# Attention loads of a fused attention and expert kernel issued one or two slots later in program order

## Chip, core and metric

The kernel runs on one core of one Trainium2 chip. The metric is the device time of one execution in microseconds (us), given as the median of several runs. Matrix products run on TensorE (PE in the profile), elementwise work on VectorE (DVE), ScalarE (ACT) and GpSimd (POOL). SyncE (SP) computes nothing here: it issues almost all DMA transfers, one after the other in program order, and an issue that has to wait holds up every issue behind it.

## What is computed

The reference is a chunked attention followed by two products of gated linear layers without activation functions:

```python
for c in range(nc):                      # 24 chunks of 32 queries, per batch (4) and head (8)
    q_c = q[:, :, c_start:c_end]
    k_full = np.concatenate([mem_k, k_ctx], axis=2)   # 8 memory keys, then 16 left, 32 own, 8 right
    v_full = np.concatenate([mem_v, v_ctx], axis=2)
    scores = scale * np.matmul(q_c, k_full.transpose(0, 1, 3, 2))
    scores = scores - np.max(scores, axis=-1, keepdims=True)
    a = np.exp(scores)
    a = a / (np.sum(a, axis=-1, keepdims=True) + 1e-09)
    out[:, :, c_start:c_end] = np.matmul(a, v_full)
x = attention output as 3072 tokens x 512
y = (((x @ w1) * (x @ w2)) @ w3) @ w_out           # 512 -> 1024 -> 512
result = ((y @ w_a) * (y @ w_b)) @ moe2_w_out      # 512 -> 1536 -> 512
```

All of it is float32. The dense products use operands split into a high and a low part and three passes.

## The kernel before

**Stages.** The first stage (up to about 81 us) decodes w3 and w_out, which arrive as raw words, and multiplies them into one matrix (`wps`, two halves of 32 products each, lines 566 to 603). The second stage goes over six tiles of 512 tokens (`ti`, line 705): for each of eight blocks `m` the products psA and psB with w1 and w2 (`ab_step`), then psY with the folded matrix. Beside it, the weights w_a and w_b are decoded, combined and stored to DRAM (`c_weights`, tiles `co`, `wc`). The third stage, from about 535 us on, is the second expert layer, a product with seven multiplications (`seven`) and the output product.

**Attention** has 16 units `u` (line 284). A unit is cut into steps, and each has a slot number: `BASE[u]` plus an offset. Per unit: `a_k` (line 110) loads the keys to `kraw`, `a_q` (line 120) the queries to `q`, `a_v` (line 129) the values to `v` in four DMAs (eight in the first unit of a batch), all on SP. `a_keys` (line 146) copies `kraw` into overlapping windows `kw` on DVE. `a_scores` (line 160) is the product `sc` on PE, `a_max` the row maximum `mx` on DVE, `a_exp` (line 196) 16 exponentials on ACT, `a_norm` the division on DVE and POOL, `a_trans` and `a_pt` the transposition `pt` and its copy, `a_pv` (line 237) the product `xp` with `v`, and `a_x` (line 256) the split of its result into `xt` (lines 99 and 102). Every one of `kraw`, `kw`, `q` and `v` has a single buffer. So q(u+1) can be loaded only after the scores of u have been computed, k(u+1) only after the copy of the keys of u, and v(u+1) only after the product xp(u).

**Order.** The order is written out by hand. `at` (line 281) puts steps into the list `todo[slot]`, and `attn_slot` (line 312) emits the next slot's steps, in the order of that list. In the first stage a slot is emitted every second product from `g` 9 of half 0 on: slots 0 to 6 in half 0, slots 7 to 22 in half 1. After the slot, `w_tick` (line 432) may follow: it decodes a weight block and issues loads of raw weights for as long as a buffer is free (`w_load`, line 350; tiles `raw`, sources `in_w3a`, `in_w3b`, then `in_w`). In half 0 this happens at `g` 0, 2, 4, 6, 8 and 9. In the second stage `between` (line 640) emits the due slots and then one `w_tick`, or one step of `c_weights`, whose loads (line 464, `in_wab`) and stores (line 493) are on SP as well. Within a slot's list, entries stand in the order in which the loop over `u` made them.

The framework adds the waits. Beside those for data and buffers, there is one for the eight completion semaphores that the DMAs of SP and ACT take in turn: a DMA whose semaphore still belongs to an unfinished transfer, eight issues back, waits for that.

Of the kernel before, what the change touches and what calls it, by code (L numbers as in the profile page):

```python
# [45 lines left out]
def tile_attention_moe(  # L46
# [60 lines left out]
    def new_batch(u):  # L107
        return NE * u % NG == 0
# [11 lines left out]
    def a_q(u):  # L120
        if u >= NA:
            return
        q = qs[u] = att.tile([P, NE, 4 * GQ], F32, tag="q", bufs=1, name="q")
        src = qt[2 * NE * u : 2 * NE * u + 2 * NE]
        nc.sync.dma_start(
            out=q, in_=src.rearrange("(e r) d h q -> (r d) e (h q)", r=2)
        )

    def a_v(u):
        if u >= NA:  # L130
            return
        for r in range(2):
            for e in range(NE):
                src = vw[2 * NE * u + 2 * e + r]
                kd, x = src.ap
                if new_batch(u):
                    mem = bass.AP(src.tensor, src.offset, [[kd[0], NMEM], [0, NC], x])
                    nc.sync.dma_start(out=v[D * r : D * r + NMEM, e, :, :], in_=mem)
                win = bass.AP(
                    src.tensor,  # L140
                    src.offset + NMEM * kd[0],
                    [[kd[0], KEYS - NMEM], [CHUNK * kd[0], NC], x],
                )
                nc.sync.dma_start(out=v[D * r + NMEM : D * r + D, e, :, :], in_=win)
# [51 lines left out]
    def a_exp(i):  # L196
        def stage_of(u):
            sc, t, mx, sm = soft[u]
            for a in range(2 * i, 2 * i + 2):
                for r in range(2):  # L200
                    nc.scalar.activation(  # L201
                        t[:, a, r, :],
                        sc[:, r, a, :],
                        AF.Exp,
                        bias=mx[:, r, a : a + 1],
                        scale=SCALE,
                        accum_out=sm[:, a, r : r + 1],
                    )

        return stage_of  # L210

    def a_norm(e):
        def stage_of(u):
            t, mx, sm = soft[u][1:]
            t, sm = t[:, 4 * e : 4 * e + 4], sm[:, 4 * e : 4 * e + 4]
            nc.vector.tensor_scalar_add(sm, sm, 1e-9)
            nc.vector.reciprocal(sm, sm)  # L217
            nc.gpsimd.tensor_tensor(  # L218
                t, t, sm[:, :, :, None].to_broadcast([GQ, 4, 2, KEYS]), ALU.mult
            )  # L220

        return stage_of
# [52 lines left out]
    BASE = [0, 6, 13, 23, 29, 36]  # L275
# [5 lines left out]
    def at(s, *stages):  # L281
        todo.setdefault(s, []).extend(stages)

    for u in range(NA):
        t0, t1, t2, t3 = SLOTS.get(u, (6, 7, 8, 9) if u < NX else (5, 5, 6, 7))
        for s, stage_of in (
            (t0, a_trans),
            (t1, a_pt),
            (t3, a_x),
            (t2, a_pv),  # L290
            (t2, lambda u: a_v(u + 1)),
            (0, a_scores),
            (0, lambda u: a_q(u + 1)),
            (int(u > 0), a_max),
            (2, a_norm(0)),
            (2 + (u > 0), a_norm(1)),
            (int(u > 0), a_exp(0)),
            (int(u > 0), a_exp(1)),
            (2 * (u > 0), a_exp(2)),
            (2 * (u > 0), a_exp(3)),  # L300
        ):
            at(BASE[u] + s, (stage_of, u))
        if u > 0:
            at(BASE[u] - 3, (a_keys, u), (a_k, u + 1))
    at(0, (a_v, 0))
    NEED = []
    for i in range(NT1):
        u = -(-TT * (i + 1) // (NE * GQ)) - 1
# [721 lines left out]
```

## Time and profile before

| | us |
|---|---|
| median of 3 runs (1075.88 to 1077.11) | 1076.02 |
| the profiled execution's own time | 1074.61 |
| its span, first to last instruction | 1072.8 |
| PE busy | 1055.9 |
| DVE busy | 452.1 |
| ACT busy | 443.3 |
| POOL busy | 233.3 |

A busy PE is not PE at its peak, since ends of matmuls are modelled; stretches in which PE is not busy are real gaps. An entry such as `[1.30 <-DVE w_f L378]` says that the engine was idle for 1.30 us before this instruction, until DVE had written `w_f` in line 378. `SPq` is the queue of SP: its times are those of issuing, and a transfer lands later.

### The profile page before, as it was taken

The page shows a single profiled execution, that of the slowest core. Times are in us where ns is not written, and L with a number is a line of the kernel's source. Part 1 is how long each engine was busy: PE and PEld are TensorE (multiplying, and loading weights), DVE is VectorE, ACT ScalarE, POOL GpSimd, SP SyncE. Part 2 cuts the span into 40 slices and gives each one's busy share as a digit, 9 for nine tenths or more (in the row PEclk, how much of TensorE's full clock was granted, in tenths as well). Part 3 has the DMA queues.
Part 4 walks back from the last instruction along what each step waited for, and adds up shares of the span by engine and source line. Part 5 has one row for each costly group of instructions (what it writes and reads, how often), then busy time and mean ns, then how long its engine had stood idle before and what let it go on. Part 6 is the DMA issues. An engine that isn't in the chain of part 4 may idle for free.

```text
span 1072.8 us, 18442 instructions
## 1 busy us (share of the span) xinstructions
PE 1055.9 (98%) x7442; PEld 844.5 (79%) x7442; DVE 452.1 (42%) x751; ACT 443.3 (41%) x1153; POOL 233.3 (22%) x228
## 2 busy tenths in 40 slices
PE   9999899999999999999999999999999999999998
PEld 3447688888888888888888888888888888888886
DVE  4667644435435435346643434432322253223310
ACT  6777754426636543535433343332222232222210
POOL 0102312202303302212033222112233202222210
PEclk9999999999999999999999999999999999999999
DMA  9966464454454462263555554523344434433311
GB/s 366 315 174 185 132 186 142 130 164 149 150 187 116 141 188 91 104 235 138 196 200 210 202 182 158 186 97 148 137 151 178 158 111 141 172 139 138 137 40 39
DMA packets 62341, 172.02 MB, mean 160 GB/s; under 512 B 6320, under 2 KB 21552, under 8 KB 56368
## 3 DMA queue, kind: packets, MB, share of 16 engines
q1 hardware_dynamic: 51680, 104.75, 30.2%
q0 software_dynamic: 10368, 66.06, 17.0%
q8 instruction: 58, 0.95, 0.4%
q14 instruction: 27, 0.22, 0.1%
q10 hardware_dynamic: 208, 0.04, 0.0%
HBM read 137.27 MB, written 33.55 MB: 159 GB/s over the span
## 4 chain that ended last, share of the span: by engine, by line
PE 86%; DVE 1%; DMA 1%; ACT 0%; issue 0%; POOL 0%; SPq 0%; ACTq 0%; POOLq 0%
PE ps L816 31%; PE ops L90 18%; PE psY L90 12%; PE psB L90 11%; PE psA L90 10%; PE xp L90 2%; PE sc L90 1%; PE pt L229 1%; DMA raw<-in_wab 1%; DVE x L102 0%; DVE tmp L670 0%; POOL g L635 0%; ACT x L99 0%; POOL t L218 0%; DVE xt L102 0%
## 5 line engine op out<-in xcount | busy, mean ns | idle before, releaser
L816 PE MATMUL ps<-x,w 128*128 128x512 f32 x1512 | 348.7, 389 | 0.3 <-ACT tmp L828 0.3
L816 PEld LDWEIGHTS ps<-x,w 128*128 128x128 f32 x1512 | 283.6, 188 | 60.1 <-ACT tmp L828 1.4
L833 DVE TENSOR_TENSOR tmp<-ps,tmp 128x512 f32<-128x512 f32 x108 | 74.6, 691 | 260.7 <-PE ps L816 230.6
L90 PE MATMUL psA<-xt,w 128*128 128x512 f32 x576 | 140.9, 393 | 3.8 <-DVE w L408 3.0
L90 PE MATMUL psB<-xt,w 128*128 128x512 f32 x576 | 140.0, 392 | 0.0
L90 PE MATMUL psY<-g,wo 128*128 128x512 f32 x576 | 136.0, 392 | 0.3 <-POOL g L635 0.3
L635 POOL TENSOR_TENSOR g<-gv,g 128x512 fp32r<-128x512 f32 x48 | 65.0, 1354 | 301.5 <-ACT g L634 301.5
L828 ACT ACTIVATE tmp<-ps 128x512 f32<-128x512 f32 x108 | 64.5, 597 | 157.5 <-PE ps L816 157.5
L90 PEld LDWEIGHTS psA<-xt,w 128*128 128x128 f32 x576 | 107.0, 188 | 28.0 <-DVE w L408 3.8
L90 PEld LDWEIGHTS psY<-g,wo 128*128 128x128 f32 x576 | 107.0, 188 | 23.1 <-POOL g L635 0.8
L90 PEld LDWEIGHTS psB<-xt,w 128*128 128x128 f32 x576 | 107.2, 188 | 22.5
L700 POOL DMA_DIRECT2D w<-wc x72 | 39.6, 552 | 373.3 <-PE ps L816 373.2
L90 PE MATMUL ops<-wo,g 128*128 128x512 f32 x504 | 118.6, 389 | 0.0
L90 PEld LDWEIGHTS ops<-wo,g 128*128 128x128 f32 x504 | 94.6, 188 | 19.6
L839 ACT ACTIVATE g<-tmp 128x512 fp32r<-128x512 f32 x66 | 40.7, 633 | 140.2 <-DVE tmp L838 140.2
L840 POOL TENSOR_TENSOR g<-tmp,g 128x512 fp32r<-128x512 f32 x66 | 84.0, 1291 | 20.8 <-ACT g L839 19.7
L201 ACT ACTIVATE t<-sc,mx 96x64 f32<-96x64 f32 x256 | 75.3, 316 | 25.0 <-DVE mx L193 23.4
L90 PE MATMUL ops<-fo,g 128*128 128x512 f32 x288 | 68.2, 389 | 0.0
L90 PEld LDWEIGHTS ops<-fo,g 128*128 128x128 f32 x288 | 54.1, 188 | 11.2
L218 POOL TENSOR_TENSOR t<-t,sm 96x512 f32<-96x512 f32 x32 | 37.2, 1163 | 104.6 <-DVE sm L217 100.3
L90 PE MATMUL wps<-w_f 128*128 128x512 f32 x128 | 57.6, 600 | 1.9 <-DVE w_f L378 1.9
L201 ACT ACTIVATION_READ_ACCUMULATOR t<-sc,mx 96x1 f32 x256 | 53.9, 211 | 0.0
(65 smaller groups left out, 870.3 us busy)
## 6 DMA issues: line engine op xcount, KB each, us to landing
w<-wc POOLq DMA_DIRECT2D x36, 1024.0 KB, 7.0
w<-wc POOLq DMA_DIRECT2D x36, 768.0 KB, 5.1
wc<-co SPq DMA_DIRECT2D x84, 256.0 KB
raw<-in_wab SPq DMA_DIRECT2D x24, 512.0 KB
v<-in_vw SPq DMA_DIRECT2D x64, 168.0 KB
kraw<-in_kt SPq DMA_DIRECT2D x16, 512.0 KB
raw<-in_w SPq DMA_DIRECT2D x16, 512.0 KB
raw<-in_w3a SPq DMA_DIRECT2D x6, 1024.0 KB
```

Source lines behind the costliest of these rows:

```text
L90: nc.tensor.matmul(o, lhsT=l, rhs=r, start=first, stop=last)
L201: nc.scalar.activation(t[:, a, r, :], sc[:, r, a, :], AF.Exp, bias=mx[:, r, a : a + 1], scale=SCALE, accum_out=sm[:, a, r : r + 1],)
L218: nc.gpsimd.tensor_tensor(t, t, sm[:, :, :, None].to_broadcast([GQ, 4, 2, KEYS]), ALU.mult)
L229: nc.tensor.transpose(pt[:, a // 4, a % 4, :], t[:, a].rearrange("p r k -> p (r k)"), id_sb)
L635: nc.gpsimd.tensor_tensor(g2[:, 1, :], gv, g2[:, 0, :].bitcast(F32), ALU.subtract)
L700: nc.gpsimd.dma_start(out=t[:, c0:c1].bitcast(F32), in_=src[:, c0:c1])
L816: nc.tensor.matmul(ps, lhsT=w[:, i, a, k, :], rhs=xs[i][:, b, k, :], start=first and n == 0, stop=n == 5, skip_group_check=not first,)
L828: nc.scalar.activation(z, ps, AF.Copy)
L833: nc.vector.tensor_tensor(z, ps, y, ALU.add)
L839: nc.scalar.activation(g2[:, 0, :], z, AF.Copy)
L840: nc.gpsimd.tensor_tensor(g2[:, 1, :], z, g2[:, 0, :].bitcast(F32), ALU.subtract)
```

## The change

Three calls change their place in the list of slots, and nothing else changes. The query load of unit u+1 moves from slot `BASE[u]` to `BASE[u] + 1`, or `+ 2` for u > 0. The value load moves from slot `BASE[u] + t2` to `BASE[u] + t2 + 1`, or `+ 2` for u > 1. The key load moves from `BASE[u] - 3` to `BASE[u] - 2`.

```diff
@@ -288,9 +288,7 @@
             (t1, a_pt),
             (t3, a_x),
             (t2, a_pv),
-            (t2, lambda u: a_v(u + 1)),
             (0, a_scores),
-            (0, lambda u: a_q(u + 1)),
             (int(u > 0), a_max),
             (2, a_norm(0)),
             (2 + (u > 0), a_norm(1)),
@@ -301,7 +299,10 @@
         ):
             at(BASE[u] + s, (stage_of, u))
         if u > 0:
-            at(BASE[u] - 3, (a_keys, u), (a_k, u + 1))
+            at(BASE[u] - 3, (a_keys, u))
+            at(BASE[u] - 2, (a_k, u + 1))
+        at(BASE[u] + 1 + (u > 0), (a_q, u + 1))
+        at(BASE[u] + t2 + 1 + (u > 1), (a_v, u + 1))
     at(0, (a_v, 0))
```

## Rows read from the trace of the kernel before

**Rows 1.** Waits of PE, 0 to 200 us: us in total, times, longest.
```profile
PE psA L90 <- DVE w L408: 3.0, 2, 2.2
PE pt L229 <- DVE xt L102: 2.5, 1, 2.5
...
PE psY L90 <- POOL g L635: 0.3, 1, 0.3
```

**Rows 2.** Waits of SP's queue over the whole span, same columns.
```profile
SPq L144 <- PE xp L90: 54.1, 23, 13.5
```

**Rows 3.** Timeline of SP's queue, 30 to 41 us: start, us, line, transfer, count.
```profile
30.08 0.39 SPq L125 DMA_DIRECT2D q<-in_qt  x1
...
38.27 0.27 SPq L138 DMA_DIRECT2D v<-in_vw  x1
40.10 0.32 SPq L144 DMA_DIRECT2D v<-in_vw  x1
40.52 0.36 SPq L357 DMA_DIRECT2D raw<-in_w3b  x1
```

**Rows 4.** Waits of SP's queue, 28 to 50 us.
```profile
SPq L138 <- DMA raw<-in_w3b: 3.8, 2, 3.2
...
SPq L144 <- DMA q<-in_qt: 1.5, 1, 1.5
```

**Rows 5.** Windows, busy us by engine; the last three columns: PEclk, DMA share, GB/s.
```profile
41.00:43.00 2.00, 0.70 (x40) 0.54 (x27) 1.97 (x3) 0.01 (x1) 0.00 (x0) 1.00 0.96 250
43.00:46.00 3.00, 3.00 (x8) 1.33 (x8) 1.56 (x3) 1.31 (x9) 0.00 (x0) 1.00 0.97 392
```

**Rows 6.** Timeline of PE, 39 to 58 us.
```profile
39.27 0.83 PE L229 MATMUL pt<-id_sb,t 96*128 96x96 f32 x8
40.22 1.18 PE L90 MATMUL sc<-kw,q 64*32 64x64 f32 x96
42.71 5.42 PE L90 MATMUL wps<-w_f 128*128 128x512 f32 x12 [1.30 <-DVE w_f L378]
...
57.50 0.85 PE L229 MATMUL pt<-id_sb,t 96*128 96x96 f32 x8 [2.50 <-DVE xt L102]
```

**Rows 7.** Timeline of DVE, 43 to 57 us.
```profile
43.17 1.21 DVE L192 TENSOR_REDUCE mx<-sc 96x16 f32<-96x1024 f32 x1
...
56.40 0.96 DVE L102 TENSOR_TENSOR xt<-xp,xt 128x768 fp32r<-128x768 f32 x1 [1.32 <-ACT xt L99]
```

**Rows 8.** Windows: PE, PEld, DVE, ACT, POOL, PEclk, DMA share, GB/s.
```profile
44.70:58.60 13.90, 11.40 (x125) 5.79 (x125) 7.62 (x11) 13.90 (x43) 2.08 (x2) 1.00 0.74 233
```

**Rows 9.** Windows at the end, same columns.
```profile
1066.00:1068.00 2.00, 1.82 (x9) 1.16 (x7) 1.21 (x2) 0.68 (x2) 0.00 (x0) 1.00 0.32 119
...
1070.00:1071.00 1.00, 0.00 (x0) 0.00 (x0) 0.00 (x0) 0.00 (x0) 0.00 (x0) 0.63 0.21 78
```

**Rows 10.** Timeline of SP's queue, 67 to 77 us.
```profile
67.45 1.94 SPq L144 DMA_DIRECT2D v<-in_vw  x4
71.53 4.90 SPq L357 DMA_DIRECT2D raw<-in_w  x3
```

**Rows 11.** Timeline of PE, the third unit's xp.
```profile
77.50 1.60 PE L90 MATMUL xp<-p,v 64*64 64x32 f32 x96
```

**Rows 12.** The chain that ended last, in order of time, 131 to 138 us.
```profile
131.08 0.40 SPq L125
...
131.57 6.63 DMA raw<-in_wab
```

**Rows 13.** Timeline of SP's queue in the steady part.
```profile
258.35 1.94 SPq L144 DMA_DIRECT2D v<-in_vw  x4
...
263.60 7.99 SPq L493 DMA_DIRECT2D wc<-co  x4
```

**Rows 14.** Timeline of PE in the steady part, the next xp.
```profile
280.29 1.60 PE L90 MATMUL xp<-p,v 64*64 64x32 f32 x96
```

**Rows 15.** Windows: ACT is the fourth busy column.
```profile
110.00:120.00 10.00, 10.00 (x134) 8.36 (x133) 4.62 (x10) 10.00 (x43) 2.52 (x2) 1.00 0.59 160
```

## Prediction

> **What bounds the kernel now.** I read the page's busy times first: PE is busy for 1055.9 us of a span of 1072.8 (the table above), so nothing that leaves PE's gaps alone changes the time. Next, PE's waits. Everything that the attention loads could touch lies in the first 150 us, and it is little: 3.0 us for split weights (`w`, line 408), 2.5 us before the second transposition, 0.3 us before psY [rows 1], and 1.30 us before the second half of the fold [rows 6]. Third, SP's own waits: its issues of `v` stood for 54.1 us behind xp [rows 2], with other loads and stores queued behind them. That wait is what the change shortens, but it is SP's, and PE pays only where something behind it comes too late. So two lists have to be made: which late transfers become earlier, and which attention loads are now themselves too late. Because SP issues in order, a move by a slot means nothing unless other SP issues lie between the old place and the new one.
>
> **The change part by part.** No instruction is added or removed: 15 q loads, 14 k loads and 72 DMAs of v change places with weight loads and with stores.
>
> *Query load of the second unit, q(1).* In the list it stood ahead of the eight DMAs of v(0), in slot 0; now it is in slot 1. Between the two lie v(0) and the `w_tick` of `g` 9, which issues the last `in_w3b` load of 1 MB. Before, q(1) went out at 30.08 and the `in_w3b` load at 40.52 [rows 3]. The gap between them is v(0): with eight semaphores in turn, its last two DMAs waited for transfers eight issues back, at 38.27 for an `in_w3b` load and at 40.10 for q(1) itself [rows 3, 4]. So q(1) took 10.0 us from issue to landing, and landed just before PE needed it at 40.22 [rows 6]: it had almost no slack. In the new order the eight DMAs of v(0) move up one semaphore; the last waits for that same `in_w3b` load and goes at about 38.3. Then the 1 MB load goes at about 38.65, and q(1) at 39.1, that is 9 us later than before, behind 1 MB.
>
> When does it land? Three prices. By bytes alone: ahead of it and with it go 0.17 MB of v, 1.05 MB and 0.39 MB, 1.61 MB together. Before, the same start (v at 40.10, `in_w3b` at 40.52) was followed by 250 GB/s for 2 us and then 392 GB/s [rows 5], that is 0.50 MB in the first 2 us and the other 1.11 MB in 2.8 us more, at 45.8; a start 1.85 us earlier makes 44.0. From above: q(1)'s own 10.0 us gives 49.1. The nearest row is the pair of loads at 131 us: a q load issued at 131.08 and a 0.5 MB load at 131.57, which landed 6.63 us later, at 138.20 [rows 12]; that is 7.1 us for 0.9 MB from the first issue, and 0.7 MB more at 392 GB/s is 1.8 us: 38.3 + 8.9 = 47.2. I take 46.0, between bytes alone and that row.
>
> What it costs: PE ends the first transposition at 40.10 and then waits until 46.0. sc(1) ends at 47.2 instead of 41.4. The 1.30 us of waiting for `w_f` are swallowed. The row maximum, which DVE could begin at 43.17 [rows 7], begins at 47.3: 4.1 us later. From there ACT is the path: it is busy for all of 44.7 to 58.6 [rows 8], exponentials and weight scaling in program order, and at its end stands the split of xp(0), for which DVE waits at 56.40 [rows 7] and PE at 57.50 [rows 6]. So PE, which has a reserve of 2.50 us there, is late by the 4.1 us of ACT. Behind 57.50 I find no reserve: the `wps` products, xp and sc follow one another without a wait, and the weight pipe of ACT and DVE is emitted between the same steps. **+4.1 us** (bounds: +2.1 with 44.0, +7.2 with 49.1).
>
> *The clock.* While PE waits from 40.10 to 46.0, the granted clock can fall. It stayed at 1.00 through the gap of 2.50 us [rows 6, 8]; but after the last matmul, which ended at 1067.8, it was 0.63 on average in 1070 to 1071 [rows 9], so it went from 2.4 to 1.2 GHz about 2.4 us after PE had stopped. At half speed sc(1) takes up to twice its 1.18 us, and it lies on the path; the fold's products behind it are covered by the reserve before the second transposition. 0 to +1.2, I take **+0.5**. The Trainium skill, page "TensorE: Matmul & The Clock Gate", section "HAM oscillation — how this bites in real kernels", says that waiting for a load between bursts of matmuls throttles the next burst; by the gap of 2.50 us alone the sum would leave out the 0.5, by that rule it stays. The end of the trace agrees with the rule.
>
> *v(2).* It moves behind the `in_w` load of `g` 9, which waits for a buffer until 71.53 [rows 10]. It goes out from 71.9 instead of 67.45, its third DMA, which xp(2) needs for its first products at 77.50 [rows 11], at about 73.0. All of these times shift by the delay above alike, so 4.5 us remain for it. With the 6.63 us of [rows 12] it would be 2.1 us late; it is a third of that load's size, so 0 to +2.1, I take **+0.5**.
>
> *Loads that come earlier.* The first two `in_wab` loads stood behind q(6) until 131.57; now they go ahead of it. ACT's wait for them ends, and with it the 0.3 us before psY [rows 1, 12]: **-0.3**. The other waits of PE there, 3.0 us for `w`, stay: ACT is busy through all of 110 to 120 [rows 15], and no load holds it.
>
> *All other moves cost nothing.* q(2), v(1) and k(2) wait for sc(1), xp(0) and the key copy in either order. In the steady part v is issued at 258.35 and first read at 280.29 [rows 13, 14]; behind at most two of the stores that begin at 263.60 it goes before 268, and even the 10.0 us of q(1) bring it in by 278. If that cover went, PE would wait at xp in each of the later units.
>
> **Sum:** +4.1 + 0.5 + 0.5 - 0.3 = +4.8 us. The profiled execution took 1074.61, with 1.8 us around its span of 1072.8, and lies 1.4 us under the median of 1076.02; I add to the median: **1080.8 us**. A change within 0.2% (2.15 us) is about what a measurement of this kernel can't tell from none.
>
> **Rivals.**
> - *The clock holds.* The row for it is the 2.50 us gap with a clock of 1.00. Then the sum is +4.3, 1080.3. Against it stands the end of the trace. Chance 0.12.
> - *q(1) is hidden.* If q(1) lands by 42, sc(1) ends by 43.2 and only the -0.3 is left: 1075.7. This needs the `in_w3b` load to let it overtake, or to be issued well before 38. The landing of q(1) at 40.10 behind other loads speaks against it. It is also the case in which SP's order does not change as I read it. Chance 0.12.
> - *Faster: weights come earlier.* If the waits for `w` came from `in_w` loads held behind q and k, the 3.0 and 0.3 us of [rows 1] would go: 1076.0 - 3.3 = 1072.7. It decides if those loads go out more than a few tenths of a microsecond after their buffers are free. A busy ACT [rows 15] speaks against it. Chance 0.04.
> - *v(2) is later still.* With the full 2.1 us, and q(1) by the row of 131 us (+5.3) and the clock's 1.2: 1076.0 + 8.3 = 1084.3. Chance 0.06.
>
> **How the numbers follow.** The forecast has 0.66. Its own range goes from bytes alone (+2.1 - 0.3) to the row of 131 us (+5.3 + 1.2 + 0.5 - 0.3): 1077.8 to 1082.7. Range: 1077.2 to 1083.3, which holds the forecast and the first rival, 0.78, and about half of the last; the hidden q(1) and the faster case stay outside. Slower by over 0.2% means over 1078.2: 0.66 + 0.12 + 0.06, less 0.04 for the low end of the forecast, is 0.80. Same: 0.12 + 0.04 = 0.16. Faster: 0.04.
>
> **What the new profile would show.** SP: the last `in_w3b` load near 38.7 and q(1) behind it near 39. PE: a gap of about 6 us before the second sc, ended by a DMA of q, and a granted clock under 1.00 after it; the second transposition near 62. A short wait for v before xp(2), the `in_wab` loads before q(6), no wait before psY. From there on everything shifted alike. I am wrong if sc(1) begins before 43, if the shift at 57.50 is not there at 165 us, or if PE waits for v or q in the steady part.

## Result and profile after

The changed kernel takes 1082.53 us (median of 4, 1082.24 to 1083.13); the kernel before, run beside it, 1076.57 (median of 4, 1075.88 to 1079.33). The ratio is 1.0053 [1.0038, 1.0069]: slower by about 6 us, inside the range, on the side that had 0.80, and 1.2 us more than the forecast's +4.8. The profiled execution of the changed kernel took 1083.13 us with a span of 1081.4, that is 8.5 us more than the profiled execution of before (1074.61, span 1072.8). Why the two traces differ by more than the medians comes out further down.

All line numbers behind the change are one higher: line 408 of before is 409 here, 357 is 358. First PE's waits in the first 200 us, in the form of [rows 1] (us in total, times, longest), after:

```profile
PE sc L90 <- DMA q<-in_qt: 5.8, 1, 5.8
PE psA L90 <- DVE w L409: 3.0, 2, 2.2
...
PE xp L90 <- ACT p L235: 1.1, 1, 1.1
PE xp L90 <- DMA v<-in_vw: 0.9, 1, 0.9
PE pt L229 <- DVE xt L102: 0.6, 1, 0.6
```

The first row is new, the largest, and it is q(1). Also new are the two at xp; the 3.0 us for split weights have stayed, the 2.5 us before the second transposition have shrunk to 0.6, and the 0.3 us before psY are gone. Beyond 200 us PE waits once for 0.3 us, as before. What SP's issues of `v` had waited behind xp, 54.1 us [rows 2], is now:

```profile
SPq L144 <- PE xp L90: 18.1, 10, 7.3
```

So the change does what it was written to do: 36 us of this wait are gone, and none of them was PE's. SP as a whole waits no less for it. All rows of this view add up to 929 us before and 942 after, since waits have moved to other issues, to the stores of `co` above all (before, then after):

```profile
SPq L493 <- DVE co L102: 82.2, 46, 6.8
SPq L494 <- DVE co L102: 125.0, 51, 9.3
```

What the 36 us were exchanged for stands in the timeline of SP's queue, after (start, us, line, transfer, count), to be held against [rows 3, 10]:

```profile
39.06 0.32 SPq L144 DMA_DIRECT2D v<-in_vw  x1
39.48 0.36 SPq L358 DMA_DIRECT2D raw<-in_w3b  x1
39.93 0.40 SPq L125 DMA_DIRECT2D q<-in_qt  x1
...
76.10 0.33 SPq L358 DMA_DIRECT2D raw<-in_w  x1
76.52 1.72 SPq L144 DMA_DIRECT2D v<-in_vw  x4
...
134.31 0.89 SPq L465 DMA_DIRECT2D raw<-in_wab  x2
140.22 0.38 SPq L125 DMA_DIRECT2D q<-in_qt  x1
```

q(1) goes out behind the 1 MB load instead of 10 us ahead of it; v(2) goes out behind an `in_w` load; the `in_wab` loads have passed q(6). PE's timeline, after, shows what that does:

```profile
39.04 0.82 PE L229 MATMUL pt<-id_sb,t 96*128 96x96 f32 x8
45.69 1.95 PE L90 MATMUL sc<-kw,q 64*32 64x64 f32 x96 [5.82 <-DMA q<-in_qt]
...
62.06 0.85 PE L229 MATMUL pt<-id_sb,t 96*128 96x96 f32 x8 [0.59 <-DVE xt L102]
...
83.28 0.30 PE L90 MATMUL xp<-p,v 64*64 64x32 f32 x2 [1.15 <-ACT p L235]
84.51 2.48 PE L90 MATMUL xp<-p,v 64*64 64x32 f32 x94 [0.93 <-DMA v<-in_vw]
86.92 3.78 PE L90 MATMUL wps<-w_f 128*128 128x512 f32 x4
90.17 4.10 PE L90 MATMUL psA<-xt,w 128*128 128x512 f32 x12
94.20 1.19 PE L90 MATMUL sc<-kw,q 64*32 64x64 f32 x96
```

Against [rows 6], the second transposition is 62.06 - 57.50 = 4.56 us late. The third unit's xp begins at 83.28 instead of 77.50 [rows 11], 5.78 late: 1.2 us were added, and the releaser is ACT. ACT in turn had waited, here in its own timeline, after:

```profile
81.33 0.67 ACT L373 ACTIVATE raw<-raw 128x512 f32<-128x512 f32 x1 [1.97 <-DMA raw<-in_w]
```

This is the `in_w` load issued at 76.10, right ahead of v(2); it took 5.2 us. The same instruction of before waited 0.46 us, for a load issued at 71.53 [rows 10] that was there by 75.24, 3.7 us later:

```profile
75.24 0.68 ACT L372 ACTIVATE raw<-raw 128x512 f32<-128x512 f32 x1 [0.46 <-DMA raw<-in_w]
```

Then, after, xp(2) waits 0.93 us for v(2) itself, and from 85 us on everything on PE takes long: four `wps` products 3.78 us, where four took 1.91 at 62.75. The windows, after (PE, PEld, DVE, ACT, POOL; then PEclk, DMA share, GB/s), say why:

```profile
38.00:44.00 6.00, 1.87 (x11) 0.97 (x9) 4.31 (x6) 2.75 (x6) 0.09 (x1) 1.00 0.65 222
44.00:50.00 6.00, 4.32 (x99) 2.91 (x100) 1.39 (x2) 0.77 (x5) 0.00 (x0) 0.50 1.02 372
...
85.00:91.00 6.00, 6.00 (x80) 3.31 (x73) 1.29 (x3) 1.62 (x4) 0.00 (x0) 0.50 0.96 283
```

The granted clock is 0.50, 1.2 instead of 2.4 GHz, once from 44 us on, within the wait for q(1), and once more after the two waits at xp(2); before has 1.00 in both places. The sc product at 94.20 is 9.14 us later than its counterpart in PE's timeline of before:

```profile
81.34 0.49 PE L90 MATMUL psA<-xt,w 128*128 128x512 f32 x1 [0.32 <-ACT xt L99]
82.34 2.79 PE L90 MATMUL psA<-xt,w 128*128 128x512 f32 x11 [0.51 <-DVE xt L102]
85.06 1.19 PE L90 MATMUL sc<-kw,q 64*32 64x64 f32 x96
```

So the sum of the traces is 4.56 (q(1), up to the transposition) + 1.22 (ACT's wait for `in_w`) + 0.93 (v(2)) + 2.43 (the rest, over the stretch at half speed) = 9.14. The 2.43 is a net figure: the two waits of before ahead of psA, 0.83 us, are gone, so the slowed products themselves took about 3.3 us more. And ACT's wait is no cost of its own in this trace: the other 94 products of xp began when v(2) had landed, at 84.51, however early the first two might have run. About 0.6 us come back before the third stage, half of it the wait before psY. The end is 8.6 us later in span.

### The profile page after: what moved, and what is told of

Its sections match the earlier page's. It is cut to its first block, busy times and chain, and to the rows that moved or that the text cites. A ratio compares the mean times of both kernels' runs of the same rounds, so it can differ in the third digit from the quotient of the medians.

```text
span 1081.4 us, 18436 instructions
## 1 busy us (share of the span) xinstructions
PE 1061.6 (98%) x7442; PEld 847.7 (78%) x7442; DVE 451.6 (42%) x751; ACT 443.7 (41%) x1153; POOL 234.1 (22%) x228
## 4 chain that ended last, share of the span: by engine, by line
PE 86%; DVE 1%; ACT 0%; issue 0%; ACTq 0%
PE ps L817 31%; PE ops L90 18%; PE psY L90 12%; PE psB L90 11%; PE psA L90 11%; PE xp L90 2%; PE sc L90 1%; PE pt L229 1%; DVE x L102 0%; DVE tmp L671 0%; ACT x L99 0%; DVE kw L154 0%; DVE w L409 0%; DVE tmp L834 0%; ACT tmp L893 0%
## 5 line engine op out<-in xcount | busy, mean ns | idle before, releaser
L90 PEld LDWEIGHTS ops<-fo,g 128*128 128x128 f32 x288 | 54.1, 188 | 11.2
L90 PE MATMUL wps<-w_f 128*128 128x512 f32 x128 | 60.9, 628 | 0.2 <-DVE w_f L379 0.2
L635 ACT ACTIVATE g<-gv 128x512 fp32r<-128x512 f32 x48 | 30.4, 634 | 59.4 <-DVE gv L634 59.4
```

The lines of the kernel that those rows point to most:

```text
L90: nc.tensor.matmul(o, lhsT=l, rhs=r, start=first, stop=last)
L635: nc.scalar.activation(g2[:, 0, :], gv, AF.Copy)
```

## Experiments

The theory: q(1) and v(2) each come too late, from separate causes, and all other moves are free. The rivals: one cause only; a cost spread over the later units; the clock, not the waits, as the greater part. The medians of before beside each run are given, since they come from other chips than the ones above: the first four runs share one chip, the last four another, and their medians of before, 1075.60 and 1075.68, agree.

**q(1) put back, v left moved**

```diff
-        at(BASE[u] + 1 + (u > 0), (a_q, u + 1))
+        at(BASE[u] + 2 * (u > 0), (a_q, u + 1))
```

> The changed kernel with q(1) alone back in slot 0, ahead of v(0) and of the last in_w3b load; v(2) stays behind the in_w load. Theory (two separate late loads): the gap of 5.8 us before the second sc and the first stretch at half clock go, and with them 4.6 us; what began at the third xp stays: 1.2 us of ACT waiting for in_w, 1.0 us for v, 2.4 us at half clock, less 0.6 before psY. Span about 1072.8 + 4.0 = 1076.8 us, 3 to 4 us over before. Rival (one cause: the first gap shifts the loads, and the second stall only follows from it): PE does not wait for v either, span about 1072.2, within 1 us of before.

Measured: 1078.36 us (1076.96 to 1081.57) against 1075.60, ratio 1.003 [1.0017, 1.0043]. PE's timeline of this run, at the third xp:

```profile
80.16 0.30 PE L90 MATMUL xp<-p,v 64*64 64x32 f32 x2
81.20 1.87 PE L90 MATMUL xp<-p,v 64*64 64x32 f32 x94 [0.75 <-DMA v<-in_vw]
```

The wait for v(2) stays without the late q(1), so it is a cause by itself. ACT's wait for `in_w` stays too, 1.60 us, though here it holds up nothing: PE reaches xp(2) late anyway in this trace, after a stretch at half speed from 57 to 63 us that followed its 2.52 us wait before the second transposition. That stretch was expected of no theory; it comes back below. Of the 2.8 us between the medians this trace shows 1.3: from the start of xp(2) to the next `wps` product it takes 2.84 us, where the run with both loads put back takes 1.54, and the clock stays at 1.00 behind it.

**v(2) put back, q left moved**

```diff
-        at(BASE[u] + t2 + 1 + (u > 1), (a_v, u + 1))
+        at(BASE[u] + t2 + (1, 0, 2)[min(u, 2)], (a_v, u + 1))
```

> The changed kernel with v(2) alone back in the slot of xp(1), ahead of the in_w load; q(1) stays behind the last in_w3b load. Theory (two separate late loads): the gap of 5.8 us before the second sc stays, with one stretch at half clock, and no wait for v at the third xp: 4.6 - 0.6, span about 1076.8 us. Rival (one cause, the first gap): nearly all of the loss stays, span 1079 us or more, with a second stretch at half clock.

Measured: 1079.97 us (1078.46 to 1080.26) against 1075.60, 1.0043 [1.003, 1.0056]. PE's timeline:

```profile
45.50 1.95 PE L90 MATMUL sc<-kw,q 64*32 64x64 f32 x96 [5.75 <-DMA q<-in_qt]
...
81.88 1.60 PE L90 MATMUL xp<-p,v 64*64 64x32 f32 x96
```

The wait for q(1) is whole, and xp(2) runs in one piece with no wait. So q(1) is worth about 4.4 us (1079.97 - 1075.60) and v(2) about 2.8 (1078.36 - 1075.60). Together that is 7.2 where the whole change costs 6.0, which the intervals allow.

**Both put back, all other moves kept**: the two edits above in one kernel.

> The changed kernel with q(1) and v(2) both back in their old places; the 13 other units keep the new slots. Theory: all other moves are free, and the in_wab loads that now go ahead of q(6) take 0.3 to 0.6 us off psY: span about 1072.2 us, time within 1 us of before or up to 0.6 us under it. Rival (the later moves cost too, by transfers that collide in the steady part): 2 us or more over before, with PE waits for v or q after 100 us.

Measured: 1075.70 us (11 runs, 1073.72 to 1076.54) against 1075.60, 0.9999 [0.999, 1.0008]. The 14 key loads, the 14 later query loads and the value loads of all later units, moved as in the change, cost nothing that can be measured (the interval is 1 us to either side); the rival of a cost spread over the later units falls. Two of the change's moves carry the whole loss.

**q(1) alone moved, in the kernel before**

```diff
-            (0, lambda u: a_q(u + 1)),
+            (int(u == 0), lambda u: a_q(u + 1)),
```

> The kernel before with q(1) alone moved to slot 1, behind v(0) and the last in_w3b load. Theory: sc(1) at about 45.7, the second transposition 4.6 us later, one stretch at half clock, everything behind shifted: span about 1072.8 + 4.6 = 1077.4 us. Rival (the first gap is absorbed by slack further on): under 2 us over before. Rival (one cause): 8 us over before.

Measured: 1080.65 us (1077.69 to 1081.37) against 1075.60, 1.0048 [1.0036, 1.0061]. PE's waits of this run, 0 to 200 us:

```profile
PE sc L90 <- DMA q<-in_qt: 5.5, 1, 5.5
...
PE psY L90 <- POOL g L635: 1.0, 1, 1.0
```

One moved load out of 15 gives most of the change's loss. The wait before psY is here, and it is missing in the changed kernel and with both put back: so one of the later moves removes it. That it is the `in_wab` loads passing q(6) fits, but no run moves them alone.

**q(1) behind v(0), but ahead of the 1 MB load** (v(2) put back too)

```diff
-        at(BASE[u] + 1 + (u > 0), (a_q, u + 1))
-        at(BASE[u] + t2 + 1 + (u > 1), (a_v, u + 1))
-    at(0, (a_v, 0))
+        if u > 0:
+            at(BASE[u] + 2, (a_q, u + 1))
+        at(BASE[u] + t2 + (1, 0, 2)[min(u, 2)], (a_v, u + 1))
+    at(0, (a_v, 0), (a_q, 1))
```

> As the kernel with both loads back, but q(1) stands behind the eight DMAs of v(0) and still ahead of the last in_w3b load. This splits what made q(1) late: the wait of v(0)'s DMAs for their semaphores, or the 1 MB in front. Theory (the semaphores hold the issue until about 39.4; the 1 MB adds some 1.5 us more): q(1) is issued at about 39.4 and lands at 43 to 44, PE waits 3 to 4 us before the second sc, the second transposition comes 1.5 to 2.5 us later than before, time 1.5 to 3 us over before. Rival (it is the 1 MB alone): q(1) lands by 42, time within 1 us of before. Rival (the issue alone): the whole 4.6 us, as with the load in front.

Measured: 1077.38 us (12 runs, 1075.09 to 1078.97) against 1075.68, 1.0014 [1.0003, 1.0025]. SP's timeline of this run:

```profile
38.55 0.32 SPq L144 DMA_DIRECT2D v<-in_vw  x1
38.97 0.40 SPq L125 DMA_DIRECT2D q<-in_qt  x1
39.46 0.41 SPq L359 DMA_DIRECT2D raw<-in_w3b  x1
```

and PE's:

```profile
42.44 1.58 PE L90 MATMUL sc<-kw,q 64*32 64x64 f32 x96 [2.67 <-DMA q<-in_qt]
```

It is the completion semaphores that hold back the issue (SP's longest wait for an `in_w3b` load ahead of these DMAs is 3.7 us here, 3.2 in [rows 4]): the last DMA of v(0) cannot go before 38.55, and q(1), behind it, not before 38.97, 8.9 us later than before [rows 3]. That alone makes sc(1) 42.44 - 40.22 = 2.2 us late. The `in_w3b` load in front adds the other 3.25 us (45.69 - 42.44): q(1) goes 0.96 us later still, and 1 MB at the 372 GB/s of the window above is 2.8 us. More than I had expected of it, and in time the greater share (1079.97 - 1077.38 = 2.6 us, from two chips, against 1.7).

**v(2) later still, behind two `in_w` loads** (q(1) put back)

```diff
-        at(BASE[u] + 1 + (u > 0), (a_q, u + 1))
-        at(BASE[u] + t2 + 1 + (u > 1), (a_v, u + 1))
+        at(BASE[u] + 2 * (u > 0), (a_q, u + 1))
+        at(BASE[u] + t2 + (1, 2, 2)[min(u, 2)], (a_v, u + 1))
```

> The kernel with q(1) back, and v(2) one slot later still, behind two in_w loads instead of one. Theory (xp(2) waits for v(2), which waits in SP's order for an in_w buffer): SP issues v(2) at about 77 to 78 instead of 73.7, PE waits for v before the third xp 3 us or so longer than the 0.8 us seen with one load in front, time 2 to 4 us over the kernel with q(1) alone back; but ACT's wait for the first in_w load, 1.60 us there, is shorter again, under 0.7 us, since no v load runs beside it. Rival (the loss came from the in_w load that v slows down, not from v): no more than the kernel with q(1) alone back.

Measured: 1082.55 us (1080.49 to 1083.31) against 1075.68, 1.0066 [1.0051, 1.008]. SP's timeline, then PE's, then ACT's:

```profile
71.61 2.99 SPq L358 DMA_DIRECT2D raw<-in_w  x2
74.69 1.73 SPq L144 DMA_DIRECT2D v<-in_vw  x4
```

```profile
80.19 0.27 PE L90 MATMUL xp<-p,v 64*64 64x32 f32 x2 [1.59 <-DMA v<-in_vw]
82.39 2.78 PE L90 MATMUL xp<-p,v 64*64 64x32 f32 x94 [1.93 <-DMA v<-in_vw]
```

```profile
75.34 0.70 ACT L373 ACTIVATE raw<-raw 128x512 f32<-128x512 f32 x1 [0.47 <-DMA raw<-in_w]
```

With v(2) 3.1 us behind the first `in_w` load instead of 0.42 us, ACT's wait for that load is back at 0.47 us, the value of before: v(2) right behind it had stretched the load from 3.7 to 5.2 us. Being behind is not the point, though. In the run with v(2) alone put back, the four DMAs go out 4.1 us ahead of the load, as in before, and the wait is 0.60 us. In the run with both put back they go out 3.1 us ahead of it (SP's timeline, then ACT's), and the load takes 4.6 us:

```profile
68.48 1.94 SPq L144 DMA_DIRECT2D v<-in_vw  x4
71.58 4.89 SPq L358 DMA_DIRECT2D raw<-in_w  x3
```

```profile
76.19 0.69 ACT L373 ACTIVATE raw<-raw 128x512 f32<-128x512 f32 x1 [1.36 <-DMA raw<-in_w]
```

So in these traces the load is slow when v(2) is issued close to it, on either side. And v(2) itself costs PE 3.5 us in this run, with a stretch at half speed. So the rival, in which the slowed `in_w` load makes the loss, falls: that wait is gone and the time is higher. One slot more in the same direction more than doubles the price of this move (6.9 us against 2.8).

**The gaps filled** (both moves put back). Two idle products, whose results nothing uses, stand in each of the two gaps of over 2 us that the kernel before has too.

```diff
+    def fill(n, rhs):
+        d = psa.tile([GQ, 2, 512], F32, tag="sc", name="fill")
+        for _ in range(n):
+            mm(d[:, 0, :], id_sb, rhs, True, True)
...
+                    if g == 5:
+                        fill(2, w3k[8].bitcast(F32)[:GQ])
...
+                if nstep[0] == 12 and i == 8 and j == 0:
+                    fill(2, rhs.bitcast(F32)[:GQ, 0, 0, :])
```

> The kernel with both loads back, and two idle matmuls of 96 x 512 (about 1.7 us together, into a spare buffer, their result is not used) in each of PE's two gaps of over 2 us that every version has: before the second transposition and inside the seventh psA. Theory (the spread between executions, and part of what one trace shows against another, is the clock falling to half in these gaps in some executions): no stretch at half clock after the start, span about 1072.2 us, median 1 to 2 us under before and a spread of under 1 us. Rival (the spread has another cause): median and spread as in the kernel without them, 1075.7 us and 1073.7 to 1076.5.

Measured: 1073.86 us (median of 11 runs, 1073.42 to 1074.72) against 1075.68 (23 runs, 1073.43 to 1079.34), 0.9986 [0.9974, 0.9997]. A twelfth execution took 2754.24 us at a granted clock of 1.0; what held it up is not known, and it is left out of these figures. The windows of the run with both put back, without and then with the filling (same columns as above):

```profile
58.00:61.00 3.00, 3.00 (x7) 0.68 (x5) 2.70 (x5) 0.48 (x2) 0.00 (x0) 0.50 0.51 175
...
126.00:129.00 3.00, 2.70 (x10) 2.21 (x11) 2.77 (x4) 1.02 (x3) 1.38 (x1) 0.51 0.79 216
```

```profile
58.00:61.00 3.00, 3.00 (x101) 1.71 (x100) 2.82 (x5) 0.47 (x2) 0.00 (x0) 1.00 0.61 175
...
126.00:129.00 3.00, 3.00 (x19) 2.57 (x18) 2.66 (x5) 1.40 (x3) 0.06 (x1) 1.00 1.01 318
```

Without the filling PE's timeline has these waits:

```profile
56.88 0.85 PE L229 MATMUL pt<-id_sb,t 96*128 96x96 f32 x8 [2.47 <-DVE xt L102]
...
126.30 2.07 PE L90 MATMUL psA<-xt,w 128*128 128x512 f32 x4 [2.22 <-DVE w L409]
```

Both end with half the clock. The gap of 2.50 us that kept its clock in the trace of before [rows 6, 8] is this same gap, and in other executions it loses it. With the gaps filled, the clock stays at 1.00, these 11 runs spread over 1.3 us, where the 11 without the filling spread over 2.8 and the 23 of before over 5.9, and the kernel is faster than before by about 1.8 us (0.03 to 0.26%). The operands come no sooner by it: the second transposition begins at 57.00 us with the filling and at 56.88 without.

**The gap before q(1) filled** (v(2) put back): five of the same idle products ahead of the first transposition.

```diff
-        at(BASE[u] + t2 + 1 + (u > 1), (a_v, u + 1))
+        at(BASE[u] + t2 + (1, 0, 2)[min(u, 2)], (a_v, u + 1))
...
+                    if g == 15:
+                        fill(5, w3k[0].bitcast(F32)[:GQ])
```

> The kernel with v(2) alone back (q(1) late) and five idle matmuls of 96 x 512 (4.3 us, result not used) ahead of the first transposition, so that PE is busy for most of the gap before the second sc. Theory (the clock's share of that gap is the slower sc, 0.5 us, since the rest lies under the wait before the second transposition): no stretch at half clock in 40 to 55 us, sc(1) still begins at about 45.5, time 0.3 to 1 us under the kernel with q(1) late. Rival (the clock is most of the loss): 2 us or more under it. Rival (the fill itself delays the first transposition's successors): over it.

Measured: 1079.26 us (1078.17 to 1080.42) against 1075.68, 1.0037 [1.0023, 1.0052]. PE's timeline and the windows around it:

```profile
45.05 1.19 PE L90 MATMUL sc<-kw,q 64*32 64x64 f32 x96 [1.20 <-DMA q<-in_qt]
...
60.58 0.85 PE L234 MATMUL pt<-id_sb,t 96*128 96x96 f32 x8 [2.12 <-DVE xt L102]
```

```profile
45.00:50.00 5.00, 4.95 (x105) 2.87 (x106) 1.39 (x2) 2.21 (x15) 0.00 (x0) 1.00 0.99 364
```

The clock stays at 1.00 and sc(1) takes 1.19 us instead of 1.95, but q(1) is as late as ever. The time is 0.7 us under that of the same kernel without filling (1079.97), from runs on two chips whose intervals overlap; so the clock's share of this loss is small, and the rival that gave it the greater part falls for q(1). For v(2) it stays open: the clock is 2.43 of the 4.58 us behind q(1)'s shift in the trace of after, and nothing of the 1.3 us in the first experiment's, and no run fills that gap.

## Why the prediction was right, and where it was not

**q(1): right, step by step.** The last DMA of v(0) was put at 38.3 and went at 39.06; q(1) at 39.1, and it went at 39.93, behind the 1 MB load as forecast; its landing at 46.0, and sc(1) began at 45.69. The row maximum was to begin 4.1 us late and ACT to carry that to the second transposition: the row maximum began 4.54 us late and the transposition 4.56, the clock's share included. With v(2) put back, 4.4 us are left, and putting this load back too takes them away (ratio 0.9999), so this is shown, not only argued. The step that made it was the reading that q(1) had landed at 40.10 for use at 40.22: a load that looks ten microseconds early in the list was just in time. With both loads put back, sc(1) even waits 0.4 us for it.

**The clock, first place: right.** +0.5 was taken for sc(1) at half speed. It took 0.77 us more, and 4.1 + 0.5 = 4.6 stands against the measured 4.56. The clock fell later than the 2.4 us read off the end of before: it was 1.00 up to 44 us, 4.1 us after the first transposition had ended. By the rule of the Trainium skill, page "TensorE: Matmul & The Clock Gate", section "HAM oscillation — how this bites in real kernels", a wait for a load between bursts throttles the next one, and the trace agrees with 0.50 behind the wait of 5.82 us.

**v(2): right that it was late, and mis-sized.** The step was "v(2), +0.5", scaled down from the 0.5 MB load of [rows 12] because v(2) is "a third of that load's size". That holds for one of its four DMAs, 168 KB against 512; the four are 672 KB, more than that load. Three things were off. First, the price of landing: PE was held up by 1.22 + 0.93 = 2.15 us at xp(2), the upper bound and not a quarter of it. The four DMAs were issued from 76.52 to 78.24 and the products that waited for them began at 84.51, at least 6.3 us after the issue: here the four came little sooner than the 0.5 MB load of [rows 12] with its 6.63, and that row's own duration was the price to take. Second, I asked only who waits for v(2), and not what v(2) does to the load ahead of it; during 1.22 of those 2.15 PE waited for ACT, which waited for `in_w`, though v(2), landing when it did, would have held xp(2) up as long without that. Third, I priced the clock for the first new gap and not for the second, which is worth 2.43 us net in that trace. So not everything behind the second transposition shifted alike, as forecast: 4.56 us there had become 9.14 at the sc product of 94.20. And "no reserve" behind 57.50 overlooked the 0.83 us of waits ahead of psA, which covered part of that stretch. By itself the move costs 2.8 us in the median.

**In_wab and psY: right in sign.** The wait of 0.33 us went, and the trace regains 0.6 us. It is too little for the medians to show, and which of the later moves did it was not isolated.

**All other moves at nothing: right.** With the two restored, the ratio is 0.9999. In the steady part v went at 270.22 and was read at 288.81, with the cover that was claimed.

**The sum: right partly by an offset.** In the two traces the loss is 8.5 us, not 4.8. The medians differ by 6.0, mostly because the profiled execution of before was a lucky one, 2.0 us under its median of 1076.57 (that of after is 0.6 over its own): it had no stretch at half speed before its end. And the parts do not add: by themselves q(1) costs 4.4 us (4.6 were forecast) and v(2) 2.8 (0.5), 7.2 together. That the sum of 4.8 came within 1.2 us of the measured 6.0 with v(2) this far off is in part luck. The 23 later runs of before spread from 1073.43 to 1079.34 us, and the kernel with both loads put back, which takes the same time, stays between 1073.42 and 1074.72 in 11 of 12 runs once its two gaps are filled; so what separates the median from the best runs is mostly these stretches. I had seen that the profiled execution lay 1.4 us under the median and did not ask why. What the clock took from before it could not take twice from the changed kernel, whose gap at the second transposition has shrunk to 0.59 us; this is an argument from the traces, which no run isolates. The rival in which the clock holds fell, as did the two in which q(1) is hidden or the weights come earlier. The measured 1082.53 lies between the forecast and the last rival, a v(2) that is later still (1084.3). Of that rival, the full lateness of v(2) came true and the later q(1) did not.

## What to carry to other kernels

On a queue that issues in order, the cost of moving a load is read from the issues between its old and its new place and from the slack between its landing and its first use; most loads here had microseconds of it, and the two that had none, both in the first stage, made the whole loss. A long wait of an issuing queue is no cost until something behind it is late, so shorten it only where that is so, and leave such first loads where they are. And before adding a difference to a median, look at the spread of the runs: a gap at which the clock falls in some executions and not in others hides in one trace and shows in the next, and filling two of them with idle products gained 1.8 us here, where no order of loads that was tried gained anything.

## What was unexpected of the hardware

- **Gaps of 2.2 to 2.5 us cost the clock in some executions and not in others.** The same waits, 2.47 and 2.22 us, were followed by 0.50 and 0.51 in the run with both moves put back, and 2.50 and 2.2 us by 1.00 in the trace of before. In that one run the second stretch stretched four psA products from 1.19 to 2.07 us. The gap of 2.2 us stands in nine of the ten traces, and the clock fell at it in four; the gap of about 2.5 us stands in four, and it fell in three. What decides from one execution to the next was not tried.
- **A load can be slowed by one issued after it.** `in_w` took 5.2 us with four DMAs of v 0.42 us behind it (4.9 in a second trace), and 3.7 to 3.9 us with them 3.1 us behind or 4.1 us ahead. In one trace they went out 3.1 us ahead of it, and it took 4.6 us. The Trainium skill, page "DMA: Bandwidth & Descriptors", section "Queues, rings and completion order", says that transfers of one issuing engine need not complete first in, first out. No run here shows that: `in_w` was slowed but still came first, at 81.33 against 84.51 for v. By which mechanism v slows it stays open.
